# Fewer of the ten resident d_ff blocks for the early token chunks, weight conversion on another schedule, its clamp on VectorE

## The chip, the cores and the metric

One Trainium2 chip, one core. The metric is device time in microseconds of one execution. The time before is the median of three runs; the profile is of another single execution of the same program.

## The reference

Attention with a block-causal mask feeds a feed-forward layer with a rational activation. The weights `w_in` and `w_out` arrive as float64, everything else as float32.

```python
# q, k, v: 8 batches, 8 heads, 576 positions, 64 dims; blocks of 64 positions, block_i >= block_j
scores = (1 / sqrt(64)) * q @ k.T;  scores = where(mask, scores, -1e9)
attn = exp(scores - max);  attn = attn / (sum + 1e-9);  o = attn @ v
x = o.transpose(0, 2, 1, 3).reshape(4608, 512)          # tokens, d_model
h = x @ w_in                                            # d_ff = 2048
g = (a0 + a1*h + a2*h**2 + a3*h**3) / (1 + |b0|*|h| + |b1|*h**2 + 1e-6)
out = g @ w_out                                         # 4608 x 512 float32
```

## The kernel before

Every product is made with three matmuls of fp32r halves: each operand is split into a high part and a low part, and high x high, high x low and low x high are added up in PSUM.

**Attention** runs in 32 visits, one for each pair of heads of each batch, four visits to a batch. A visit has ten steps: five query tiles of growing key length (64 to 576 keys) for each of two heads. A step issues the score matmuls and the row maximum (`scores`); `expo` follows a step later, `transp` (division already done, transposes back into PSUM, split into halves) some ten steps later, and `pv` (the product with v) after the tiles 2 and 4. Its result is stored into a DRAM scratch `xscr`, from which the feed-forward part loads its tokens. Under a visit, `load` and `prep` fetch and transpose the next visit's q and k.

**Feed-forward** is cut into units. d_ff has 16 blocks of 128. In phase 0 a chunk has 256 tokens and a unit two blocks; in phase 1 a chunk has 512 tokens and a unit one block. Before, phase 0 takes blocks 0 to 9 for all 18 chunks (5 units each, 90 in all), phase 1 blocks 10 to 15 for all 9 chunks (6 units each, 54 in all). The weights of blocks 0 to 9 are resident in SBUF from the start on (`wpool`); those of 10 to 15 are converted into DRAM (`wscr`) and loaded when the attention's buffers are free. A unit passes `first` (24 or 12 matmuls into PSUM, and the first half of the polynomial), one unit later `recip`, then `split` (halves of g) and `second` (12 matmuls with N = 512). Phase 0 stores partial sums to `pscr`; phase 1 adds them and stores the output. The PSUM tile of `first` has one buffer in phase 0; the working tiles u, v, s have two.

**Weight conversion.** A step of `split_weights` loads 128 x 512 float64 values as pairs of 32-bit words and builds the high and the low half from their bits in `place`: an absolute value on ScalarE, a clamp on GpSimd (line 130), five bit operations on VectorE (132 to 139), a conversion of the low word on ScalarE (141), and two writes of the halves, on ScalarE and GpSimd for the resident blocks (144, 145), with DMAs for the others (147 to 149). There are 20 such steps for the resident blocks and 12 for the others. They use the working tiles u, v, s of the feed-forward part and its output staging tile `os`.

**Order.** The program interleaves by attention step. Conversions of the resident blocks stand at steps 9, 18, 27, 36 and then one at each step from 44 to 59; those of the others come at equal distances from step 80 to 230. Units begin at step 53, where the first batch's attention is complete, at a pace of a quarter of a half-unit per step for 40 steps, then evenly, so that 72 units are due at step 333. `ready` holds them behind the tokens that exist. The tile framework then orders each engine's queue by a timeline of its own, with what is ready earliest first, so an instruction can run ahead of its written place when its inputs and buffers allow it.

Lines that the prediction uses: 122 (fetch of weights), 130 to 149 (conversion), 207 (first product), 214 to 219, 224, 229 to 232 (activation), 239 and 240 (halves of g), 257 (second product), 432 to 437 (scores and maximum), 449 (exponential), 462 (division), 481 to 487 (transposes and their halves), 500 to 505 (product with v and its store).

Of the kernel before, what the change touches and what calls it, by code (L numbers as in the profile page):

```python
# [28 lines left out]
C0 = 0  # L29
# [6 lines left out]
W0 = 36  # L36
WA = 44
WD = 4
WB0 = 80
WBN = 150  # L40
UP = 25
UN = 40
# [7 lines left out]
NU = (NFA // NBU[0], NFB // NBU[1])  # L50
NCS = (NT // CTS[0], NT // CTS[1])
LP = 96
# [9 lines left out]
def attn_ffn_kernel(  # L62
# [52 lines left out]
    def split_weights(pool, f0, nf, dt):  # L115
        wih, wil, woh, wol = weight_tiles(pool, f0, nf, dt)

        def place(dhi, dlo, src, nm):

            nd, n = src.shape[1:]  # L120
            st = ffn.tile([128, 512, 2], I32, name=f"st{nm}", tag="os")
            nc.sync.dma_start(out=st.rearrange("p (d f) t -> p d (f t)", d=nd), in_=src.bitcast(I32))
            w0, w1 = st[:, :, 0], st[:, :, 1]
# [5 lines left out]
            nc.scalar.activation(out=at, in_=w1.bitcast(F32), func=AF.Abs)  # L129
            nc.gpsimd.tensor_scalar_max(at, at, WMIN)  # L130

# [6 lines left out]
            nc.vector.tensor_scalar(out=pi, in0=w0, scalar1=9, scalar2=None, op0=ALU.logical_shift_right)  # L138
# [12 lines left out]
        def steps():  # L151
            for f in range(0, nf, 2):
                cs = slice(f * 128, f * 128 + 256)
                for d in range(0, 4, 2):
                    src = w_in[d * 128:(d + 2) * 128, (f0 + f) * 128:(f0 + f + 2) * 128]
                    place(wih[:, d:d + 2, cs], wil[:, d:d + 2, cs],
                          src.rearrange("(d p) f -> p d f", p=128), f"i{f0}_{f}_{d}")
                    yield
                for d in range(f, f + 2):
                    place(woh[:, d:d + 1, :], wol[:, d:d + 1, :],  # L160
                          w_out[(f0 + d) * 128:(f0 + d + 1) * 128, :].rearrange("(d p) e -> p d e", p=128),
                          f"o{f0}_{d}")
                    yield

        return (wih, wil, woh, wol), steps()


    class Ffn:
# [26 lines left out]
        def first(self, ph, c, u):  # L195
            wih, wil, _, _ = self.w[ph]
# [5 lines left out]
            for j in range(NBU[ph]):  # L202
                f = NBU[ph] * u + j
                fs = slice(f * 128, (f + 1) * 128)
# [39 lines left out]
        def second(self, ph, c, u):  # L244
            _, _, woh, wol = self.w[ph]
            gh, gl = self.g.pop((ph, c, u))
            nu = NU[ph]
# [4 lines left out]
            for j in range(NBU[ph]):  # L252
                f = NBU[ph] * u + j
                for m in range(nm):
                    ms = slice(m * 128, (m + 1) * 128)
                    for i, (g, w) in enumerate(((gl, woh), (gh, woh), (gh, wol))):
                        nc.tensor.matmul(self.o[m], lhsT=g[:, j, ms], rhs=w[:, f, :],  # L257
                                         start=(u == 0 and j == 0 and i == 0),
                                         stop=(u == nu - 1 and j == NBU[ph] - 1 and i == 2))
            if u == nu - 1:  # L260
# [17 lines left out]
        def steps(self):  # L278
            units = [(ph, c, u) for ph in range(2) for c in range(NCS[ph]) for u in range(NU[ph])]
            l1, l2, l3 = LAG  # L280
            for i in range(len(units) + l3):
# [9 lines left out]
                if i < len(units):  # L291
                    ph, c, u = units[i]
                    self.first(ph, c, u)
                    if u == NU[ph] - 1:
# [14 lines left out]
    with ExitStack() as actx:  # L309
# [239 lines left out]
        for _ in range(C0):  # L549
            next(wsteps)  # L550
# [17 lines left out]
        NWA, NWB = 2 * NFA, 2 * NFB  # L568
        wdone = C0
        WSTEPS = [0] * C0 + [(W0 * (i + 1)) // 4 for i in range(4 - C0)] + [WA + WD * i // 4 for i in range(NWA - 4)]  # L570

        LAST = ALAG3 + 3
        there = [(6 * NPAIR + LAST, 1)] if G1 else []
        there += [((b + 1) * KB + LAST, ((b + 1) * S) // CT) for b in range(B)]
        E0, E1, U1 = there[0][0], there[-2][0], there[-2][1] * NU[0] * 2 - HOLD
        for step in attn_steps():

            wgoal = sum(step >= x for x in WSTEPS) + max(0, min(NWB, NWB * (step - WB0) // WBN))
            while wdone < wgoal:
                next(wsteps if wdone < NWA else wstepsB)  # L580
                wdone += 1
            while there and step >= there[0][0]:
                ff.ready = there.pop(0)[1]
            if step >= E0:
                goal = min(ff.ready * NU[0] * 2, (step - E0 + 1) * UP // 100 if step < E0 + UN else
                           (UN * UP // 100 + (U1 - UN * UP // 100) * (step - E0 - UN + 1) // (E1 + KB - E0 - UN)))
# [45 lines left out]
```

## Time and profile before

| | |
|---|---|
| median of three runs | 1383.16 us (1382.53 to 1386.95) |
| span of the profiled execution | 1379.1 us |
| mean granted TensorE clock | 0.974 |
| busy: TensorE matmul, weight load | 1278.1 us (93%), 1149.6 us (83%) |
| busy: VectorE, ScalarE, GpSimd | 1027.2 (74%), 909.4 (66%), 958.2 us (69%) |
| DMA | 200.84 MB, mean 146 GB/s |

The profiled execution has no run time of its own beside the span; the span runs from its first to its last instruction, and the runs' median is 4.1 us more. In the views PE is TensorE's matmul, PEld its weight load, DVE VectorE, ACT ScalarE, POOL GpSimd and SP SyncE; "L207" is line 207 of the kernel. A row of a group ends with: busy us, mean ns of one, idle time of the engine before them and what ended it. A matmul's shown duration contains its passage through the array, so neighbouring matmuls overlap; the distance of their starts is what one costs.

### The profile page before, as it was taken

The page shows a single profiled execution, that of the slowest core. Times are in us where ns is not written, and L with a number is a line of the kernel's source. Part 1 is how long each engine was busy: PE and PEld are TensorE (multiplying, and loading weights), DVE is VectorE, ACT ScalarE, POOL GpSimd, SP SyncE. Part 2 cuts the span into 40 slices and gives each one's busy share as a digit, 9 for nine tenths or more (in the row PEclk, how much of TensorE's full clock was granted, in tenths as well). Part 3 has the DMA queues.
Part 4 walks back from the last instruction along what each step waited for, and adds up shares of the span by engine and source line. Part 5 has one row for each costly group of instructions (what it writes and reads, how often), then busy time and mean ns, then how long its engine had stood idle before and what let it go on. Part 6 is the DMA issues. An engine that isn't in the chain of part 4 may idle for free.

```text
span 1379.1 us, 24416 instructions
## 1 busy us (share of the span) xinstructions
PE 1278.1 (93%) x8088; PEld 1149.6 (83%) x8088; DVE 1027.2 (74%) x2048; ACT 909.4 (66%) x2250; POOL 958.2 (69%) x1240
## 2 busy tenths in 40 slices
PE   4677899999899979999999999999989999999997
PEld 3667788999888879888998999998979888888885
DVE  5898877787778857887767777776676767676675
ACT  4766767777677756777767777776645655555553
POOL 4889987687678747777767676666556666666654
PEclk9788999999999999999999999999999999999999
DMA  9778556666556655665654555652632233333332
GB/s 216 198 196 238 146 150 166 168 166 181 148 145 150 164 151 132 165 166 153 157 140 123 154 134 122 160 127 65 213 141 77 77 123 123 122 123 123 122 113 86
DMA packets 216925, 200.84 MB, mean 146 GB/s; under 512 B 129504, under 2 KB 184800, under 8 KB 216800
## 3 DMA queue, kind: packets, MB, share of 16 engines
q1 hardware_dynamic: 216736, 199.28, 53.6%
q8 instruction: 65, 1.06, 0.3%
q14 instruction: 60, 0.49, 0.1%
q0 software_dynamic: 64, 0.00, 0.0%
HBM read 98.57 MB, written 44.04 MB: 103 GB/s over the span
## 4 chain that ended last, share of the span: by engine, by line
PE 69%; DVE 9%; POOL 9%; DMA 5%; ACT 3%; issue 3%; SPq 1%; POOLq 0%; DVEq 0%; ACTq 0%
PE h L207 25%; PE o L257 24%; PE o L500 8%; PE t L481 4%; PE s L432 3%; PE s L433 2%; PE tp L366 2%; POOL gl L240 1%; POOL p L462 1%; DMA x<-xscr 1%; POOL u L217 1%; DVE v L231 1%; DVE nm L437 1%; POOL v L216 1%; DMA xscr<-x 1%
## 5 line engine op out<-in xcount | busy, mean ns | idle before, releaser
L207 PE MATMUL h<-x,wih 128*128 128x256 f32 (+1 forms) x1872 | 415.7, 313 | 9.0 <-DMA x<-xscr 7.9
L207 PEld LDWEIGHTS h<-x,wih 128*128 128x128 f32 x1872 | 309.7, 191 | 29.1 <-issue 6.6
L207 PE MATMUL h<-x,wil 128*128 128x256 f32 (+1 forms) x936 | 290.7, 311 | 0.0
L240 POOL TENSOR_TENSOR gl<-s,gh 128x512 fp32r<-128x512 f32 x144 | 188.8, 1313 | 106.4 <-ACT gh L239 103.0
L257 PE MATMUL o<-woh,gl 128*128 128x512 f32 x576 | 232.2, 403 | 12.1 <-POOL gl L240 10.6
L257 PE MATMUL o<-wol,gh 128*128 128x512 f32 x576 | 227.7, 396 | 0.0
L257 PE MATMUL o<-woh,gh 128*128 128x512 f32 x576 | 227.7, 395 | 0.0
L437 DVE TENSOR_REDUCE nm<-s 128x1 f32<-128x288 f32 (+4 forms) x384 | 161.7, 427 | 78.4 <-PE s L436 45.2
L449 ACT ACTIVATE p<-s,nm 128x288 f32<-128x288 f32 (+4 forms) x384 | 184.9, 485 | 48.3 <-DVE nm L437 35.0
L217 POOL TENSOR_TENSOR u<-v,u 128x512 f32<-128x512 f32 x144 | 189.6, 1317 | 9.8
L216 POOL TENSOR_SCALAR v<-u,bab 128x512 f32<-128x512 f32 x144 | 118.9, 826 | 98.1 <-ACT u L214 94.6
L207 PEld LDWEIGHTS h<-x,wil 128*128 128x128 f32 x936 | 178.7, 191 | 8.7
L462 POOL TENSOR_SCALAR p<-p,rc 128x128 f32<-128x128 f32 (+3 forms) x256 | 164.8, 655 | 29.6 <-DVE rc L457 27.7
L218 DVE TENSOR_TENSOR s<-s,h 128x512 f32<-128x512 f32 x144 | 98.5, 684 | 100.1 <-ACT s L215 99.4
L432 PE MATMUL s<-kq 128*128 128x256 f32 (+3 forms) x384 | 137.3, 360 | 24.3 <-DMA kq<-hl 8.9
L224 ACT ACTIVATE v<-u,qcb 128x512 f32<-128x512 f32 x144 | 104.6, 726 | 69.6 <-POOL u L217 68.9
L214 ACT ACTIVATE u<-h 128x512 f32<-128x512 f32 x144 | 85.9, 596 | 94.2 <-PE h L207 90.1
L239 ACT CAST gh<-s 128x512 fp32r<-128x512 f32 x144 | 89.2, 623 | 82.1 <-DVE s L232 81.5
L257 PEld LDWEIGHTS o<-woh,gl 128*128 128x128 f32 x576 | 109.2, 190 | 35.5 <-POOL gl L240 14.3
L257 PEld LDWEIGHTS o<-wol,gh 128*128 128x128 f32 x576 | 109.1, 189 | 22.2
L257 PEld LDWEIGHTS o<-woh,gh 128*128 128x128 f32 x576 | 109.3, 190 | 18.9
L433 PE MATMUL s<-kq 128*128 128x256 f32 (+3 forms) x384 | 120.1, 315 | 0.0
(105 smaller groups left out, 3043.5 us busy)
## 6 DMA issues: line engine op xcount, KB each, us to landing
kq<-hl SPq DMA_DIRECT2D x64, 432.0 KB, 4.3
kq<-hl SPq DMA_DIRECT2D x64, 288.0 KB, 5.3
x<-xscr SPq DMA_DIRECT2D x56, 256.0 KB, 4.2
xscr<-x SPq DMA_DIRECT2D x32, 320.0 KB, 4.7
qr<-in_q_dram SPq DMA_DIRECT2D x64, 144.0 KB, 2.9
kr<-in_k_dram SPq DMA_DIRECT2D x64, 144.0 KB, 3.0
kq<-hl SPq DMA_DIRECT2D x64, 144.0 KB, 4.8
pscr<-os SPq DMA_DIRECT2D x18, 512.0 KB, 2.9
```

Of the source, the lines that this page charges most:

```text
L207: nc.tensor.matmul(h[:, j, :], lhsT=w[:, dc, fs], rhs=xs[dc][:, hl, :], start=(dc == 0 and i == 0), stop=(dc == 3 and i == 2))
L216: nc.gpsimd.tensor_scalar(out=vt, in0=ut, scalar1=b1, scalar2=b0, op0=ALU.mult, op1=ALU.add)
L217: nc.gpsimd.tensor_tensor(out=ut, in0=vt, in1=ut, op=ALU.mult)
L224: nc.scalar.activation(out=vt, in_=ut, func=AF.Ln, bias=qcb)
L240: nc.gpsimd.tensor_tensor(out=gl.rearrange("p j t -> p (j t)"), in0=st, in1=gh.rearrange("p j t -> p (j t)").bitcast(F32), op=ALU.subtract)
L257: nc.tensor.matmul(self.o[m], lhsT=g[:, j, ms], rhs=w[:, f, :], start=(u == 0 and j == 0 and i == 0), stop=(u == nu - 1 and j == NBU[ph] - ...
L432: nc.tensor.matmul(ps[:, :ww], lhsT=kq[:, 0, qs], rhs=kq[:, 1, c0:c0 + ww], start=True, stop=False)
L433: nc.tensor.matmul(ps[:, :ww], lhsT=kq[:, 0, qs], rhs=kq[:, 2, c0:c0 + ww], start=False, stop=not last)
L437: nc.vector.reduce_max(out=nm[:nq, j, i:i + 1], in_=ps[:nq, :w], axis=AX.X, negate=True)
L449: nc.scalar.activation(out=pt[:nq, j, c0:c0 + w], in_=banks[i][:nq, :w], func=AF.Exp, bias=nm[:nq, j, 0:1], scale=1.0, accum_out=sm[:nq, j ...
L462: nc.gpsimd.tensor_scalar(out=pt[:nq, jj, 64:n], in0=pt[:nq, jj, 64:n], scalar1=rc[:nq, jj:jj + 1], scalar2=1.0, op0=ALU.mult, op1=ALU.mult)
L500: nc.tensor.matmul(o[:, s0:w], lhsT=vblock(vv, x), rhs=pp, start=(x == 0 and i == 0), stop=(x == nb - 1 and i == 2))
```

## The change

Phase 0's units per chunk become a list: 2, 2, 3, 3, 4, 4 and then 5 for the other twelve chunks (4, 4, 6, 6, 8, 8 and then 10 blocks), 78 units in all. Phase 1 takes what is left of each pair of chunks: 12, 10 and 8 units for the first three, then 6 each, 66 in all; those of the first three chunks begin with resident blocks. Conversion steps are split into a fetch and a `place`, the fetch three attention steps ahead. Their places become a written list from step 4 to 164 for the resident blocks, and equal distances from step 176 to 312 for the others. Units are due by straight lines: 4 by step 93, 10 by step 133, 18 by step 173, 60 by step 333. The clamp moves to VectorE, and two instructions of `place`, the absolute value on ScalarE and the shift of the low word on VectorE, are pinned in the queue behind what the program has issued on their engine before them. The rest of the diff carries the unit count and the block numbers through `first`, `second` and `steps`.

```diff
@@ -26,20 +26,14 @@
 ALAG2 = 1
 LEND = 4
 RL = 3
-C0 = 0
 KQB = 3
 XB = 3
 HOLD = 6
 ALAG3 = 10
 OFFS = {5:(0,3,5)}
 G1 = 0
-W0 = 36
-WA = 44
-WD = 4
-WB0 = 80
-WBN = 150
-UP = 25
-UN = 40
+WB0 = 176
+WBN = 136
 LAG = (1, 2, 3)
 GBUFS = 2
 CBUFS = 2
@@ -47,8 +41,8 @@
 NFB = NF - NFA
 
 CTS, NBU = (CT, 512), (2, 1)
-NU = (NFA // NBU[0], NFB // NBU[1])
 NCS = (NT // CTS[0], NT // CTS[1])
+UA = (2, 2, 3, 3, 4, 4) + (5,) * 12
 LP = 96
 NL = S // LP
 QSCALE = 0.125
@@ -115,27 +109,29 @@
     def split_weights(pool, f0, nf, dt):
         wih, wil, woh, wol = weight_tiles(pool, f0, nf, dt)
 
-        def place(dhi, dlo, src, nm):
-
-            nd, n = src.shape[1:]
+        def fetch(src, nm):
+            nd = src.shape[1]
             st = ffn.tile([128, 512, 2], I32, name=f"st{nm}", tag="os")
             nc.sync.dma_start(out=st.rearrange("p (d f) t -> p d (f t)", d=nd), in_=src.bitcast(I32))
+            return st
+
+        def place(dhi, dlo, st, nd, nm):
             w0, w1 = st[:, :, 0], st[:, :, 1]
             at = ffn.tile([128, 512], F32, name=f"wa{nm}", tag="u")
             bt = ffn.tile([128, 512], F32, name=f"wb{nm}", tag="v")
             pt = ffn.tile([128, 512], F32, name=f"wp{nm}", tag="s")
             ai, bi, pi = at.bitcast(I32), bt.bitcast(I32), pt.bitcast(I32)
 
-            nc.scalar.activation(out=at, in_=w1.bitcast(F32), func=AF.Abs)
-            nc.gpsimd.tensor_scalar_max(at, at, WMIN)
-
+            tc.keep_in_program_order(nc.scalar.activation(out=at, in_=w1.bitcast(F32), func=AF.Abs))
+            nc.vector.tensor_scalar_max(at, at, WMIN)
             nc.vector.tensor_scalar(out=ai, in0=ai, scalar1=3, scalar2=0x3FFFF000,
                                     op0=ALU.logical_shift_left, op1=ALU.bitwise_and)
             nc.vector.scalar_tensor_tensor(out=bi, in0=w1, scalar=-0x40000000, in1=ai,
                                            op0=ALU.bitwise_and, op1=ALU.bitwise_or)
 
             nc.vector.tensor_scalar(out=ai, in0=bi, scalar1=-0x800000, scalar2=None, op0=ALU.bitwise_and)
-            nc.vector.tensor_scalar(out=pi, in0=w0, scalar1=9, scalar2=None, op0=ALU.logical_shift_right)
+            tc.keep_in_program_order(nc.vector.tensor_scalar(out=pi, in0=w0, scalar1=9, scalar2=None,
+                                                             op0=ALU.logical_shift_right))
             nc.vector.scalar_tensor_tensor(out=pi, in0=w1, scalar=23, in1=pi,
                                            op0=ALU.logical_shift_left, op1=ALU.bitwise_or)
             nc.scalar.activation(out=pt, in_=pt.bitcast(U32), func=AF.Copy, scale=2.0 ** -43)
@@ -153,17 +149,25 @@
                 cs = slice(f * 128, f * 128 + 256)
                 for d in range(0, 4, 2):
                     src = w_in[d * 128:(d + 2) * 128, (f0 + f) * 128:(f0 + f + 2) * 128]
-                    place(wih[:, d:d + 2, cs], wil[:, d:d + 2, cs],
-                          src.rearrange("(d p) f -> p d f", p=128), f"i{f0}_{f}_{d}")
+                    st = fetch(src.rearrange("(d p) f -> p d f", p=128), f"i{f0}_{f}_{d}")
+                    yield
+                    place(wih[:, d:d + 2, cs], wil[:, d:d + 2, cs], st, 2, f"i{f0}_{f}_{d}")
                     yield
                 for d in range(f, f + 2):
-                    place(woh[:, d:d + 1, :], wol[:, d:d + 1, :],
-                          w_out[(f0 + d) * 128:(f0 + d + 1) * 128, :].rearrange("(d p) e -> p d e", p=128),
-                          f"o{f0}_{d}")
+                    st = fetch(w_out[(f0 + d) * 128:(f0 + d + 1) * 128, :].rearrange("(d p) e -> p d e", p=128),
+                               f"o{f0}_{d}")
                     yield
+                    place(woh[:, d:d + 1, :], wol[:, d:d + 1, :], st, 1, f"o{f0}_{d}")
+                    yield
 
         return (wih, wil, woh, wol), steps()
 
+
+    def nu(ph, c):
+        return NF - 2 * UA[2 * c] if ph else UA[c]
+
+    def blocks(ph, c, u):
+        return [2 * UA[2 * c] + u] if ph else [2 * u, 2 * u + 1]
 
     class Ffn:
         def __init__(self):
@@ -193,15 +197,14 @@
                 self.x[ph, c] += [x[:, d] for d in range(nd)]
 
         def first(self, ph, c, u):
-            wih, wil, _, _ = self.w[ph]
             xs = self.x[ph, c]
             tag = f"{ph}_{c}_{u}"
             pool = self.pools[self.n % len(self.pools)]
             hp = self.hpools[self.n % len(self.hpools)]
             h = hp.tile([128, NBU[ph], CTS[ph]], F32, name=f"h{tag}", tag="a", bufs=1 if hp is ps_h else 3)
-            for j in range(NBU[ph]):
-                f = NBU[ph] * u + j
-                fs = slice(f * 128, (f + 1) * 128)
+            for j, f in enumerate(blocks(ph, c, u)):
+                wih, wil, _, _ = self.w[f // NFA]
+                fs = slice(f % NFA * 128, (f % NFA + 1) * 128)
                 for dc in range(4):
                     for i, (w, hl) in enumerate(((wih, 1), (wih, 0), (wil, 0))):
                         nc.tensor.matmul(h[:, j, :], lhsT=w[:, dc, fs], rhs=xs[dc][:, hl, :],
@@ second, steps
...
-            for j in range(NBU[ph]):
-                f = NBU[ph] * u + j
+            for j, f in enumerate(blocks(ph, c, u)):
+                _, _, woh, wol = self.w[f // NFA]
...
-            units = [(ph, c, u) for ph in range(2) for c in range(NCS[ph]) for u in range(NU[ph])]
+            units = [(ph, c, u) for ph in range(2) for c in range(NCS[ph]) for u in range(nu(ph, c))]
...
@@ -546,8 +548,6 @@
 
         wts, wsteps = split_weights(wpool, 0, NFA, F32R)
         load(0)
-        for _ in range(C0):
-            next(wsteps)
         prep(0, 0)
         prep(0, 1)
         vprep(0)
@@ -565,26 +565,27 @@
 
         KB = NPAIR * 10
         wscr, wstepsB = split_weights(dpool, NFA, NFB, F32)
-        NWA, NWB = 2 * NFA, 2 * NFB
-        wdone = C0
-        WSTEPS = [0] * C0 + [(W0 * (i + 1)) // 4 for i in range(4 - C0)] + [WA + WD * i // 4 for i in range(NWA - 4)]
+        at_ = [4, 12, 20, 28, 42, 46, 50, 54, 64, 72, 80, 88, 100, 109, 118, 127, 140, 148, 156, 164]
+        at_ += [WB0 + WBN * i // (2 * NFB) for i in range(2 * NFB)]
+        WSTEPS = sorted([(k, 1) for k in at_] + [(max(0, k - 3), 0) for k in at_])
+        wall = (x for g in (wsteps, wstepsB) for x in g)
 
         LAST = ALAG3 + 3
-        there = [(6 * NPAIR + LAST, 1)] if G1 else []
-        there += [((b + 1) * KB + LAST, ((b + 1) * S) // CT) for b in range(B)]
-        E0, E1, U1 = there[0][0], there[-2][0], there[-2][1] * NU[0] * 2 - HOLD
+        there = [((b + 1) * KB + LAST, ((b + 1) * S) // CT) for b in range(B)]
+        E0, E1 = there[0][0], there[-2][0]
+        UC = lambda n: 2 * sum(UA[:n])
+        PACE = [(E0, 0), (E0 + KB, UC(2)), (E0 + 2 * KB, UC(4)), (E0 + 3 * KB, UC(6)),
+                (E1 + KB, UC(there[-2][1]) - HOLD)]
         for step in attn_steps():
 
-            wgoal = sum(step >= x for x in WSTEPS) + max(0, min(NWB, NWB * (step - WB0) // WBN))
-            while wdone < wgoal:
-                next(wsteps if wdone < NWA else wstepsB)
-                wdone += 1
+            while WSTEPS and step >= WSTEPS[0][0]:
+                WSTEPS.pop(0)
+                next(wall)
             while there and step >= there[0][0]:
                 ff.ready = there.pop(0)[1]
             if step >= E0:
-                goal = min(ff.ready * NU[0] * 2, (step - E0 + 1) * UP // 100 if step < E0 + UN else
-                           (UN * UP // 100 + (U1 - UN * UP // 100) * (step - E0 - UN + 1) // (E1 + KB - E0 - UN)))
-                emit(max(0, goal - done))
+                (s0, u0), (s1, u1) = next(((x, y) for x, y in zip(PACE, PACE[1:]) if step < y[0]), PACE[-2:])
+                emit(max(0, min(UC(ff.ready), u0 + (u1 - u0) * (step - s0 + 1) // (s1 - s0)) - done))
 
     wB = ctx.enter_context(tc.tile_pool(name="wB", bufs=1))
     ffb = ctx.enter_context(tc.tile_pool(name="ffb", bufs=2))
```

More of the change, by code (lines that the diff above doesn't have):

```diff
@@ L244, in second @@
         def second(self, ph, c, u):
-            _, _, woh, wol = self.w[ph]
             gh, gl = self.g.pop((ph, c, u))
-            nu = NU[ph]
+            last = u == nu(ph, c) - 1
             nm = CTS[ph] // 128
@@ L256, in second @@
                     for i, (g, w) in enumerate(((gl, woh), (gh, woh), (gh, wol))):
-                        nc.tensor.matmul(self.o[m], lhsT=g[:, j, ms], rhs=w[:, f, :],
+                        nc.tensor.matmul(self.o[m], lhsT=g[:, j, ms], rhs=w[:, f % NFA, :],
                                          start=(u == 0 and j == 0 and i == 0),
-                                         stop=(u == nu - 1 and j == NBU[ph] - 1 and i == 2))
-            if u == nu - 1:
+                                         stop=(last and j == NBU[ph] - 1 and i == 2))
+            if last:
                 for k in range(nm // 2):
@@ L293, in steps @@
                     self.first(ph, c, u)
-                    if u == NU[ph] - 1:
+                    if u == nu(ph, c) - 1:
                         self.x.pop((ph, c))
```

## The prediction

> **What bounds the kernel now.** I read the busy shares first, then the busy times of six stretches with the granted clock, then the groups of instructions inside the stretches, then single visits, then single instructions. A step is the score matmul of one head of one query tile, ten steps make a visit (one pair of heads) and 320 the attention. The cuts come from the score matmuls' start times: step 0 starts at 17.5 us, step 53 at 145.9, step 173 at 515.9, and the attention's last matmuls end near 968 to 980.
>
> ```profile
> PE 1278.1 (93%) x8088; PEld 1149.6 (83%) x8088; DVE 1027.2 (74%) x2048; ACT 909.4 (66%) x2250; POOL 958.2 (69%) x1240
> ```
>
> TensorE looks like the bound everywhere. The stretches say otherwise:
>
> ```profile
> core 0: us, PE busy (x) PEld busy (x) DVE busy (x) ACT busy (x) POOL busy (x), PEclk, DMA share, GB/s
> 17.50:145.90 128.40, 92.84 (x539) 82.98 (x540) 109.53 (x260) 88.60 (x269) 109.55 (x146) 0.81 0.81 211
> 145.90:515.90 370.00, 341.70 (x2419) 315.91 (x2417) 288.82 (x624) 259.70 (x715) 276.32 (x389) 0.99 0.62 158
> 515.90:700.00 184.10, 178.44 (x1281) 165.45 (x1280) 146.95 (x318) 134.72 (x366) 141.06 (x200) 1.00 0.60 150
> 700.00:968.00 268.00, 265.57 (x1912) 247.98 (x1912) 194.73 (x435) 195.53 (x525) 182.89 (x284) 1.00 0.52 129
> 968.00:1065.00 97.00, 91.08 (x586) 82.78 (x585) 65.20 (x82) 52.96 (x88) 56.52 (x45) 0.96 0.40 143
> 1065.00:1379.10 314.10, 304.17 (x1341) 251.21 (x1339) 214.81 (x314) 172.27 (x279) 186.05 (x167) 0.99 0.34 114
> ```
>
> Take length minus busy time times clock as what TensorE loses: 53.2 us in the first row, 31.7 in the second, then 5.7, 2.4, 9.6 and 13.0. TensorE's work is nearly the same in both kernels, so the change can only win or lose in these losses. The first row holds the largest. There TensorE is not the bound: VectorE and GpSimd are both busy 85% of the time (109.5 of 128.4), and weight conversions fill them:
>
> ```profile
> L130 POOL TENSOR_SCALAR wai<-wai 128x512 f32<-128x512 f32 x9 | 15.4, 1710 | 1.5 <-ACT wai L129 1.1
> L130 POOL TENSOR_SCALAR wao<-wao 128x512 f32<-128x512 f32 x8 | 13.1, 1641 | 0.6 <-ACT wao L129 0.3
> L145 POOL TENSOR_TENSOR wil<-wpi,wai 128x512 fp32r<-128x512 f32 x9 | 11.6, 1295 | 4.4 <-ACT p L449 4.3
> L145 POOL TENSOR_TENSOR wol<-wpo,wao 128x512 fp32r<-128x512 f32 x8 | 10.2, 1270 | 0.7 <-DVE wao L137 0.5
> L134 DVE SCALAR_TENSOR_TENSOR wbi<-sti,wai 128x512 int32<-128x512 int32 x10 | 8.3, 833 | 0.0
> L132 DVE TENSOR_SCALAR wao<-wao 128x512 int32<-128x512 int32 x8 | 3.7, 468 | 1.1 <-POOL wao L130 1.1
> ```
>
> These are the first stretch's groups: 17 conversions. On VectorE there are ten such groups (the first and the last are shown) with 59.4 us, 3.5 us a conversion; on GpSimd 50.3 us, of which the clamp (L130) is 28.5, 1.68 us each. By the written schedule only 4 conversions belong before step 44; the trace shows that the planner had pulled them some 25 steps forward.
>
> **The change, part by part.** The plan after has conversions at steps 4, 12, 20, 28, 42, 46 and 50 in the first stretch (7 for 17), 13 from step 54 to 164 in the second (10 ran there before), and 12 from step 176 to 300 in the rest (4 before; one before 17.5 us). The pin holds a conversion's first instruction behind what ScalarE has already been given, so it cannot run ahead. Early chunks have 2, 2, 3, 3, 4, 4 units, so 18 units are due by step 173.
>
> ```profile
> L207 PE MATMUL h<-x,wih 128*128 128x256 f32 x29 | 6.3, 315 | 0.1
> ...
> L207 PE MATMUL h<-x,wih 128*128 128x256 f32 x484 | 96.3, 292 | 7.9 <-DMA x<-xscr 7.9
> ...
> L207 PE MATMUL h<-x,wih 128*128 128x256 f32 x685 | 135.8, 290 | 0.1
> ```
>
> With 16 of these to a unit, the first stretch has under 2 units, the second 30, the rest of the attention 43. After: 0, 18, some 44. The planner drew units about 5 ahead of their pace; after it can hardly do so before step 163, since the chunks' tokens are not there.
>
> *First stretch.* VectorE: 109.5 - 59.4 + 7 x 4.1 = 78.8 us. The 4.1 is 3.5 plus the clamp's new place, priced at 0.6 from the mean of the other one-input VectorE instructions (0.47 to 0.88 in this stretch). GpSimd: 109.6 - 50.3 + 7 x 1.28 = 68. At the same 85% VectorE needs 92 us. A visit's chain also has a length of its own:
>
> ```profile
> 17.50:34.70 17.20, 10.08 (x51) 8.18 (x52) 12.77 (x36) 11.60 (x38) 10.13 (x17) 0.92 1.00 232
> 87.50:108.70 21.20, 17.10 (x102) 15.77 (x103) 19.88 (x48) 17.10 (x54) 19.88 (x28) 0.76 0.82 210
> 108.70:136.30 27.60, 21.69 (x137) 19.88 (x135) 24.13 (x53) 18.52 (x54) 24.65 (x32) 0.81 0.86 235
> ```
>
> Visit 0, which has nobody's transposes before it, took 17.2 us; visit 3, with some three conversions, 21.2; visit 4, with more, 27.6. With 1.3 conversions a visit I take 20 us: 17.2 + 4.3 x 20 = 103, so 25 us shorter. About 5 us of unit work (43 first matmuls at 0.12) go to later: -20. Ends: 92 us (-31) and 24 a visit (-2). I take the value nearest to visit 3.
>
> *Second stretch.* Twelve units leave. A unit costs TensorE 24 x 0.120 + 12 x 0.227 = 5.6 us:
>
> ```profile
> 944.92 0.40 PE L207 MATMUL h<-x,wih 128*128 128x256 f32 x2
> 945.16 0.28 PE L207 MATMUL h<-x,wil 128*128 128x256 f32 x1
> ...
> 1109.63 0.39 PE L257 MATMUL o<-woh,gl 128*128 128x512 f32 x1
> 1109.86 0.39 PE L257 MATMUL o<-woh,gh 128*128 128x512 f32 x1
> ```
>
> and VectorE five instructions, 3.9 us:
>
> ```profile
> L218 DVE TENSOR_TENSOR s<-s,h 128x512 f32<-128x512 f32 x144 | 98.5, 684 | 100.1 <-ACT s L215 99.4
> L219 DVE SCALAR_TENSOR_TENSOR s<-s,coef,h 128x512 f32<-128x512 f32 x144 | 107.0, 743 | 2.4
> L230 DVE SCALAR_TENSOR_TENSOR u<-u,v 128x512 f32<-128x512 f32 x90 | 72.1, 802 | 27.3 <-ACT v L229 25.9 <-POOL vpl L394 0.8
> L231 DVE SCALAR_TENSOR_TENSOR v<-u,v 128x512 f32<-128x512 f32 x90 | 74.2, 824 | 1.1
> L232 DVE SCALAR_TENSOR_TENSOR s<-s,coef,v 128x512 f32<-128x512 f32 x90 | 78.1, 868 | 1.2
> ```
>
> VectorE after: 288.8 - 12 x 3.9 - 10 x 3.5 + 13 x 4.1 = 260 us; TensorE's work 338.3 - 67 = 271. VectorE is then nearly level with TensorE, and at the first stretch's 85% it sets 305 us. That is 65 shorter for 67 us of work moved to later: +2. Ends: at 90% VectorE and 94% TensorE 289 (-14), at 80% 325 (+22). So taking units away here buys almost nothing by itself: the stretch only changes its bound.
>
> *From step 173 to the attention's end.* TensorE is the bound and eight conversions are added. Between 515.9 and 700 us four conversions stand beside 5.7 us lost, between 700 and 968 none beside 2.4, so one costs (5.7 - 2.4 x 184/268) / 4 = 1.0 us. Single visits give more:
>
> ```profile
> 628.30:660.70 32.40, 29.43 (x208) 27.11 (x208) 26.64 (x57) 22.98 (x63) 25.03 (x35) 1.00 0.50 125
> 660.70:689.60 28.90, 28.90 (x223) 27.58 (x222) 22.79 (x50) 22.31 (x60) 22.07 (x33) 1.00 0.67 162
> ```
>
> The first of these, with one conversion, loses 3.0, the second, without, nothing. I take the mean over the long stretch: 8 x 1.0 = +8; ends 0 and +24.
>
> *The units that change phase.* Twelve units of 5.6 us become twelve of 24 x 0.227 = 5.45: -2. The twelve join the last phase, where VectorE (215 of 314 us) and GpSimd (186) have room. The loads ahead of use cost nothing as long as a staging buffer is free: 512 KB each, as before, under the attention's matmuls; if both are taken by a chunk's output, the fetch stands at the head of SyncE's queue and the next visit's q and k loads behind it. The end of the last phase and the join at 1024 us keep their loss.
>
> Sum: -20 + 2 + 8 - 2 = -12 us on a span of 1379.1, 1367. The runs' median, 1383.2, is 4.1 over the span of the profiled execution; so 1371.
>
> **The rivals.** *The clamp on VectorE collides with GpSimd (slower).* A one-input VectorE instruction that meets a GpSimd one takes far longer:
>
> ```profile
> 558.96 1.29 POOL L240 TENSOR_TENSOR gl<-s,gh 128x512 fp32r<-128x512 f32 x1
> 559.02 1.52 DVE L132 TENSOR_SCALAR wai<-wai 128x512 int32<-128x512 int32 x1 [0.20 <-POOL wai L130]
> 562.67 0.40 DVE L137 TENSOR_SCALAR wai<-wbi 128x512 int32<-128x512 int32 x1
> ```
>
> 1.52 us beside L240, 0.40 alone. If the clamp and the mask behind it both meet one each time, a conversion takes 2.2 us more of VectorE; in the second stretch, where VectorE is level with the bound, that is 13 x 2.2 / 0.85 = +34: span 1401, time 1405. It decides from about 0.8 us a conversion on. Against it: the mean of such instructions is 0.47 to 0.88. The Trainium skill states the same cause: its GPSIMD Engine Reference, Key points, says that GpSimd shares its SBUF interfaces with VectorE and contends with VectorE instructions in a 2-port mode or with two SBUF inputs. The trace agrees in the 1.52 against 0.40; by the rule taken strictly, with GpSimd busy 75% of the second stretch, the clamp would be dear there, and this rival would hold.
>
> *The early visits have a length of their own.* If a visit takes 24 us even with one conversion (visit 4 took 27.6 with both engines near 90%), the first term is -2: 1385 span, 1389.
>
> *VectorE and GpSimd really were all that held the early part.* Then the ends hold, -31, -14 and 0, with -2: span 1332, time 1336. For it: both engines are equally full in the first row, and the clamp's 28.5 us leave the fuller chain.
>
> *The clock.* The first row has 0.81. Fewer units could spread that into the second stretch: 271 us of work at 0.9 would need 301, just below VectorE's 305. So this adds nothing until the clock falls below 0.89. By the Trainium skill (TensorE: Matmul & The Clock Gate, What's actually happening) the clock halves after an idle window of about 3.4 us; no wait of that length is expected with TensorE busy 88%, and the second row's 0.99 at 92% agrees.
>
> **How the numbers follow.** Forecast 0.55; clamp 0.15; long visits 0.17; full gain 0.13. A change of under 0.3% (4 us) is about what a measurement of this kernel cannot tell from none. The forecast's own spread puts 0.51 of its 0.55 faster, 0.03 level and 0.01 slower; the long visits are level with 0.08 and slower with 0.09. Faster 0.64, same 0.11, slower 0.25. The range reaches to 1345, most of the way to the full gain, and to 1396, beyond the long visits and short of the full clamp rival. The likeliest case alone holds 1360 to 1382.
>
> **What would show it.** First stretch: step 53 near 120 us, with about 7 conversions, GpSimd busy under 70%. Second: step 173 near 425 us with some 18 units done and VectorE busy about 85%, TensorE near 88%. Then visits near 31 to 33 us with a conversion in most. The clamp's group on VectorE near 0.6 us. Wrong would be: step 53 not before 138 us, or the clamp and L132's successor over 1 us in the mean, or visits over 34 us after step 173.

## The result and the profile after

The changed kernel takes 1438.85 us (median of four runs, 1435.25 to 1441.69) against 1385.06 us for the kernel before: 1.039 times the time, interval 1.0361 to 1.0419. The forecast of 1371 us, its range and its sign were wrong. The profiled execution's span is 1433.5 us against 1379.1, so 54.4 us have to be found.

The busy shares of the page after:

```profile
PE 1305.9 (91%) x7944; PEld 1167.0 (81%) x7944; DVE 1038.8 (72%) x2080; ACT 912.6 (64%) x2250; POOL 897.7 (63%) x1208
```

GpSimd got 60 us of work less and VectorE 12 us more, as the diff says. Both have a smaller share than before, and still the run is longer. The same six stretches, cut at step 0, step 53, step 173, a round time, the end of the attention and the join, show where (columns as in the table before):

```profile
core 0: us, PE busy (x) PEld busy (x) DVE busy (x) ACT busy (x) POOL busy (x), PEclk, DMA share, GB/s
19.20:129.00 109.80, 83.02 (x521) 76.35 (x521) 71.50 (x205) 70.02 (x231) 55.78 (x115) 0.86 0.78 189
129.00:482.60 353.60, 302.13 (x1987) 277.81 (x1986) 266.22 (x598) 237.33 (x676) 218.42 (x347) 0.88 0.63 157
482.60:700.00 217.40, 210.70 (x1490) 195.00 (x1488) 177.46 (x392) 158.80 (x435) 152.85 (x232) 0.98 0.64 165
700.00:947.00 247.00, 234.02 (x1656) 216.57 (x1656) 186.90 (x409) 174.00 (x465) 174.27 (x248) 0.99 0.56 144
947.00:1065.00 118.00, 113.42 (x701) 102.14 (x700) 81.52 (x98) 62.91 (x105) 73.26 (x59) 0.99 0.35 123
1065.00:1433.50 368.50, 358.31 (x1579) 295.84 (x1577) 250.08 (x366) 205.18 (x331) 219.02 (x197) 0.99 0.29 95
```

The prediction's measure, length minus TensorE's busy time times its clock, gives the loss of each. It is good to some 4 us in the longest rows, since the clock has two places and is a mean over the stretch, not over TensorE's busy time.

| stretch | loss before | loss after | difference | predicted |
|---|---|---|---|---|
| steps 0 to 53 | 53.2 | 38.4 | -14.8 | -20 |
| steps 53 to 173 | 31.7 | 87.7 | +56.0 | +2 |
| step 173 to the attention's end | 8.1 | 26.2 | +18.1 | +8 |
| to the join | 9.6 | 5.7 | -3.9 | 0 |
| last phase | 13.0 | 13.8 | +0.8 | 0 |

Together +56.2. Step 0 begins 1.7 us later, and the twelve units that change phase save 12 x (24 x 0.120 - 12 x 0.227) = 1.9 us of matmuls by the prediction's distances. That makes 56.0 for the 54.4, which is within the error. So the question is the second row. Its +56.0 has two parts: TensorE's idle time grew by 23.2 us (51.5 for 28.3), and the lower clock costs 36.3 us of its busy time for 3.4, which is 32.8 more.

In that stretch VectorE is busy 266.2 of 353.6 us, 75%, and TensorE 85% at a clock of 0.88. No engine is full. The longest waits of TensorE there, after and then before (total, times, longest):

```profile
PE s L434 <- DMA kq<-hl: 11.8, 5, 4.6
PE o L502 <- DVE pt0l L489: 8.7, 5, 2.6
PE tp L368 <- DMA kr<-in_k_dram: 4.7, 4, 2.7
```

```profile
PE h L207 <- DMA x<-xscr: 7.9, 3, 3.0
PE o L500 <- DVE pt0l L487: 4.9, 4, 2.1
PE tp L366 <- ACT p L449: 3.7, 3, 1.6
```

They now belong to the steps of a visit: the copy of q and k, the transposed probabilities, the load of k. None is large by itself.

### The profile page after: what moved, and what is told of

Read it like the earlier page. It is cut to its first block, busy times and chain, and to the rows that moved or that the text cites. A ratio compares the mean times of both kernels' runs of the same rounds, so it can differ in the third digit from the quotient of the medians.

```text
span 1433.5 us, 24128 instructions
## 1 busy us (share of the span) xinstructions
PE 1305.9 (91%) x7944; PEld 1167.0 (81%) x7944; DVE 1038.8 (72%) x2080; ACT 912.6 (64%) x2250; POOL 897.7 (63%) x1208
## 4 chain that ended last, share of the span: by engine, by line
PE 68%; DVE 11%; DMA 8%; ACT 4%; POOL 3%; issue 3%; SPq 2%; POOLq 0%; DVEq 0%; ACTq 0%
PE h L210 25%; PE o L259 23%; PE o L502 8%; DMA kq<-hl 5%; PE t L483 4%; PE s L434 3%; PE s L435 3%; PE tp L368 2%; DVE nm L439 1%; DMA kr<-in_k_dram 1%; DVE pt2l L489 1%; POOL gl L243 1%; ACT p L451 1%; DVE s L221 1%; DVE u L233 1%
## 5 line engine op out<-in xcount | busy, mean ns | idle before, releaser
L210 PEld LDWEIGHTS h<-x,wih 128*128 128x128 f32 x1776 | 302.7, 194 | 34.5 <-DMA x<-xscr 3.4
L210 PE MATMUL h<-x,wil 128*128 128x256 f32 (+1 forms) x888 | 284.3, 320 | 0.0
L259 PE MATMUL o<-woh,gl 128*128 128x512 f32 x576 | 229.3, 398 | 6.1 <-POOL gl L243 5.2
L220 POOL TENSOR_TENSOR u<-v,u 128x512 f32<-128x512 f32 x144 | 192.9, 1339 | 9.7
L434 PE MATMUL s<-kq 128*128 128x256 f32 (+3 forms) x384 | 145.0, 379 | 51.6 <-DMA kq<-hl 38.5
L464 POOL TENSOR_SCALAR p<-p,rc 128x128 f32<-128x128 f32 (+3 forms) x256 | 161.7, 644 | 39.9 <-DVE rc L459 37.5
L210 PEld LDWEIGHTS h<-x,wil 128*128 128x128 f32 x888 | 172.5, 194 | 10.7
L434 PEld LDWEIGHTS s<-kq 128*128 128x128 f32 x384 | 79.0, 206 | 64.4 <-issue 42.0
L483 PE MATMUL t<-ident,p 128*128 128x128 f32 (+1 forms) x672 | 116.0, 286 | 14.7 <-ACT p L451 5.9
```

The costliest lines, as they stand in the source:

```text
L210: nc.tensor.matmul(h[:, j, :], lhsT=w[:, dc, fs], rhs=xs[dc][:, hl, :], start=(dc == 0 and i == 0), stop=(dc == 3 and i == 2))
L220: nc.gpsimd.tensor_tensor(out=ut, in0=vt, in1=ut, op=ALU.mult)
L259: nc.tensor.matmul(self.o[m], lhsT=g[:, j, ms], rhs=w[:, f % NFA, :], start=(u == 0 and j == 0 and i == 0), stop=(last and j == NBU[ph] - ...
L434: nc.tensor.matmul(ps[:, :ww], lhsT=kq[:, 0, qs], rhs=kq[:, 1, c0:c0 + ww], start=True, stop=False)
L464: nc.gpsimd.tensor_scalar(out=pt[:nq, jj, 64:n], in0=pt[:nq, jj, 64:n], scalar1=rc[:nq, jj:jj + 1], scalar2=1.0, op0=ALU.mult, op1=ALU.mult)
L483: nc.tensor.transpose(ps[:, i, :nq], src, ident[:nq, :nq])
```

## The experiments

Theories, numbered as the expectations name them: 1, the copy of q and k to its three buffers has become the bound; 2, the pins hold up queues; 3, the clamp (3a in the later runs), and 3b the conversions as a whole, lengthen VectorE's chain; 4, any edit gives a new order of instructions, and that alone costs 10 to 30 us; 5, conversions and units collide in shared tiles; 6, an early visit has a length of its own, and the units taken away had only filled it; 7, the late conversions are dear; 8, a load three steps ahead holds a staging tile too long. Each ratio is to the kernel before on the same chip at the same time and carries a 95% interval.

### One part of the change at a time

`units_only`: the kernel before with the changed units and their pace.

```
+UA = (2, 2, 3, 3, 4, 4) + (5,) * 12      # and PACE as in the change
 places: 9, 18, 27, 36, 44, 45, ... 59, then from 80 on, as before; load at the place; clamp on GpSimd; no pins
```

> The kernel before with the new unit list and pace alone (2, 2, 3, 3, 4, 4 and then 5 units); conversions at their old steps, unpinned, clamp on GpSimd. Theory 1, copy loop: the second copy of a visit's q and k halves can only be issued when the third kq buffer comes free near the end of the visit before, takes 6 to 8 us and is used at once, so a visit does not get below 26 to 29 us when units are taken away from it: 1430 to 1455 us, steps 53 to 173 take over 340 us with about 17 units. Theory 2, pinned conversions in every visit hold the queues: 1375 to 1392 us. Theory 3, clamp on VectorE: 1375 to 1392 us.

Measured 1398.1 against 1383.6, 1.0105 (1.0088 to 1.0122).

`style_only`: the changed kernel with the units, their pace and the places of the conversions as before; what is left of the change are the pins, the load three steps ahead and the clamp on VectorE.

```
-UA = (2, 2, 3, 3, 4, 4) + (5,) * 12
+UA = (5,) * 18
 places: 9, 18, 27, 36, 44, 45, ... 59, then from 80 on
+PACE = [(E0, 0), (E0 + 40, 10), (E1 + KB, UC(there[-2][1]) - HOLD)]
```

> The new way of converting (fetch ahead, two pins, clamp on VectorE) at the old steps and with the old units (5 a chunk). Theory 1: 1372 to 1398 us, since no unit is taken from a visit. Theory 2: 1410 us or more, the pins hold ScalarE and VectorE at places where 16 conversions follow each other. Theory 3: 1395 to 1415 us.

Measured 1402.4, 1.0131 (1.0114 to 1.0148).

`clamp_only`: the kernel before, one line changed.

```
-            nc.gpsimd.tensor_scalar_max(at, at, WMIN)
+            nc.vector.tensor_scalar_max(at, at, WMIN)
```

> The kernel before with the clamp on VectorE and nothing else. Theories 1 and 2: 1370 to 1387 us; 28 us of GpSimd leave the first stretch, where it is busy 85%, and VectorE gets some 10. Theory 3: 1395 us or more, the clamp's mean on VectorE near 1.2 us.

Measured 1413.6, 1.0215 (1.0199 to 1.0230).

`units_only` costs 14.5 us, `style_only` 18.8, the whole change 53.8: some 20 us are in neither alone. They belong to the new places of the conversions or to the parts meeting. The second stretch of `units_only` has the changed kernel's units and 31 us less length; below it that of `style_only`, which has 27 units and 19 conversions, since its pins hold back nine that the kernel before ran in the first stretch:

```profile
143.80:466.50 322.70, 286.69 (x1982) 258.40 (x1981) 234.53 (x560) 224.63 (x654) 225.59 (x353) 0.97 0.70 180
129.00:511.70 382.70, 345.18 (x2305) 315.55 (x2305) 312.33 (x679) 268.51 (x728) 270.45 (x380) 0.93 0.63 161
```

Their losses are 44.6 and 61.7 us for 31.7 before. So in this stretch the units alone cost 12.9 us and the new way of converting alone 30.0; the other 13 of the 56.0 come only with the whole change. Compare steps 93 to 173, `style_only` and then the changed kernel:

```profile
259.80:511.60 251.80, 239.40 (x1683) 221.79 (x1681) 199.65 (x430) 179.36 (x486) 179.35 (x257) 0.98 0.63 160
```

```profile
244.80:482.60 237.80, 204.61 (x1375) 188.45 (x1374) 176.67 (x394) 159.84 (x453) 145.22 (x231) 0.91 0.62 155
```

`style_only` does 308 matmuls more over the same 80 steps, 8.6 units or 48 us of work by the prediction's 5.6 us a unit, in only 14.0 us more (with 6 conversions for 8). Those units fill time that the changed kernel leaves idle.

### Undoing one part of the changed kernel

`after_no_pins` takes both pins away:

```
-            tc.keep_in_program_order(nc.scalar.activation(...)); tc.keep_in_program_order(nc.vector.tensor_scalar(...))
+            nc.scalar.activation(...); nc.vector.tensor_scalar(...)
```

> The changed kernel without its two pins; the planner may draw conversions forward again. Theory 1: 1425 to 1450 us, the units are missing in steps 53 to 173 as before. Theory 2: under 1415 us.

`after_clamp_pool` puts the clamp back:

```
-            nc.vector.tensor_scalar_max(at, at, WMIN)
+            nc.gpsimd.tensor_scalar_max(at, at, WMIN)
```

> The changed kernel with the clamp back on GpSimd. Theory 1 (starved visits wait for the copy into the third kq buffer): 1425 to 1445 us, the starved stretch keeps its loss. Theory 3a (the clamp on VectorE lengthens each conversion's run of VectorE instructions, between which the scores' maxima have to wait; it cost 30 us alone): 1405 to 1420 us. Theory 4 (each new order that the planner finds lies 10 to 30 us above the order of the kernel before, whatever is changed): 1415 to 1450 us with no tie to the clamp.

`fetch_at_place` loads at the conversion's own step:

```
-        WSTEPS = sorted([(k, 1) for k in at_] + [(max(0, k - 3), 0) for k in at_])
+        WSTEPS = sorted([(k, 1) for k in at_] + [(k, 0) for k in at_])
```

> The changed kernel with each fetch at its conversion's step and not three steps ahead. Theory 8 (the fetched words hold one of the two staging tiles that the chunks' outputs need): steps 173 to the attention's end lose 10 to 20 us less, 1415 to 1428 us. Otherwise 1430 to 1450 us.

Measured 1433.0 (1.0356, 1.0332 to 1.0380), 1427.7 (1.0334, 1.0307 to 1.0361) and 1428.9 (1.0322, 1.0279 to 1.0365). Each gives back 6 to 11 us of 54. None is the cause of the whole; theories 2 and 8 fall as main causes of the total. Their second stretches, in the same order, say more than the totals:

```profile
138.70:474.50 335.80, 294.01 (x1982) 265.86 (x1981) 255.82 (x580) 229.20 (x663) 209.23 (x340) 0.94 0.64 161
126.30:465.70 339.40, 291.80 (x1953) 265.02 (x1952) 253.95 (x580) 232.28 (x669) 236.66 (x359) 0.93 0.65 161
128.40:472.20 343.80, 298.47 (x1997) 273.54 (x1997) 265.33 (x602) 239.06 (x678) 219.85 (x349) 0.91 0.64 160
```

The loss there is 59.4, 68.0 and 72.2 us for 87.7, so each part of the new way of converting has a share in it, the pins the largest (28 us). The shares add up to more than the 56.0, so they overlap. Other stretches take part of it back: without pins the first stretch is 10 us longer (119.9), with the clamp on GpSimd the third (474.5 for 464.4).

### The copy of q and k (theory 1)

A fourth buffer needs space. `alias` makes it by keeping no low half of the resident output weights (its products read the high half in its place) and is the control; `alias_kqb4` and `alias_kqb4_hl2` add buffers.

```
 alias:            wol = [128, 1, DM] scratch; in second: wol = woh for f < NFA
 alias_kqb4:       -KQB = 3   +KQB = 4
 alias_kqb4_hl2:   and two buffers for hl, the copy's source
```

> The changed kernel, with the low half of w_out left out for the resident blocks (the high half is used in its place, so the output lacks that term; the same instructions run). It is the control for the next two and frees 18 KB a partition. All theories: within 12 us of the changed kernel, 1427 to 1450 us.

> As the control (low half of w_out left out for the resident blocks), with four kq buffers for three. Theory 1: the second copy of the next visit goes out before the current visit's last scores; the TensorE loss in steps 53 to 173 falls from about 105 us to under 75, and the time to 1385 to 1412 us. Theories 3a and 4: no tie to the buffer, 1425 to 1450 us.

> As the one with four kq buffers, and two buffers for the halves of q and k from which the copies are made. Theory 1, if the next link of the same chain is the halves' buffer: another 5 to 20 us less than with four kq buffers alone; if not, within 8 us of it. Theories 3a and 4: 1425 to 1450 us.

Measured 1434.7 (1.0385, 1.0353 to 1.0417), 1443.0 (1.0445, 1.0398 to 1.0492) and 1438.4 (1.0411, 1.0386 to 1.0437). The wait that theory 1 blames went down from 10.6 to 2.3 us. Waits of TensorE in the second stretch, `alias` and then `alias_kqb4`:

```profile
PE s L439 <- DMA kq<-hl: 10.6, 5, 4.0
PE o L507 <- DVE pt0l L494: 8.7, 5, 2.6
```

```profile
PE o L507 <- DVE pt0l L494: 13.2, 7, 3.2
PE h L214 <- DMA x<-xscr: 5.7, 2, 4.9
...
PE s L439 <- DMA kq<-hl: 2.3, 1, 2.3
```

The probabilities took its place, and the stretch hardly moved, 352.6 to 348.7 us:

```profile
127.20:475.90 348.70, 297.24 (x1969) 271.84 (x1969) 260.98 (x596) 234.68 (x671) 218.22 (x347) 0.90 0.62 159
```

Theory 1 falls: the wait was where the idle time showed, not why it was there.

### The conversions' chain (theories 3 and 5)

`no_dve_conv` and `before_no_dve` take every VectorE instruction out of the conversions, in both kernels. ScalarE keeps two of its three passes and GpSimd its product; in the kernel before GpSimd's clamp goes too.

```
-            the Abs on ScalarE, the clamp, the five VectorE instructions, the scaling on ScalarE
+            nc.scalar.copy(out=bt, in_=w1.bitcast(F32))
-            nc.gpsimd.tensor_tensor(..., in0=v3(pt), in1=v3(at), op=ALU.mult)
+            nc.gpsimd.tensor_tensor(..., in0=v3(bt), in1=v3(bt), op=ALU.mult)
```

> The changed kernel with each conversion cut to a copy on ScalarE and one product on GpSimd, so that VectorE has none of its seven instructions (the weights are not the reference's). Theory 3a: at 14 conversions and some 5 us each in steps 53 to 173, that stretch falls from 354 to about 285 to 305 us and the time to 1350 to 1385 us. Theory 1 and the plain length of a visit: steps 53 to 173 keep over 325 us, since a visit's own chain sets it, and the time stays over 1400 us.

> The kernel before with each conversion cut to a copy on ScalarE and one product on GpSimd (the weights are not the reference's): what all conversions cost in the old arrangement; in the new one the same cut gave 28 us. Theory 6: steps 0 to 53 fall from 128 to about 110 us, as in the changed kernel, and the rest little: 1350 to 1368 us. Theory 3b: under 1345 us.

Measured 1410.0 (1.0190, 1.0161 to 1.0219) and 1356.8 (0.9820, 0.9771 to 0.9869). Steps 0 to 53, 53 to 173 and on to the attention's end, `no_dve_conv` and then `before_no_dve`:

```profile
18.70:129.10 110.40, 81.58 (x519) 74.88 (x520) 57.17 (x171) 67.33 (x228) 52.06 (x119) 0.83 0.78 193
129.10:463.30 334.20, 293.93 (x1999) 269.40 (x1998) 214.32 (x515) 229.44 (x659) 201.48 (x346) 0.93 0.66 165
463.30:924.90 461.60, 441.88 (x3136) 411.15 (x3135) 323.86 (x724) 324.51 (x886) 308.21 (x476) 0.99 0.60 154
```

```profile
17.20:132.20 115.00, 84.03 (x521) 75.55 (x521) 57.78 (x170) 79.17 (x250) 60.97 (x127) 0.83 0.90 233
132.20:491.50 359.30, 343.09 (x2437) 319.17 (x2437) 253.10 (x576) 256.86 (x707) 246.63 (x380) 0.98 0.64 163
491.50:955.90 464.40, 457.48 (x3287) 426.32 (x3284) 337.30 (x746) 332.48 (x900) 320.29 (x483) 1.00 0.56 138
```

The part left out costs 28.9 us in the new arrangement (1438.9 - 1410.0) and 25.3 in the old (1382.1 - 1356.8): spreading the conversions out hid none of it. And without it the two kernels still stand 53 us apart, so VectorE's conversions do not explain the total, and theory 3 falls as the main cause. By stretches they do count: without them the kernels' losses in the second stretch differ by 37.8 us (60.9 and 23.1) and not 56.0, and the first stretch gains 2.6 (42.7 and 45.3) and not 14.8. The first row also says that 110 us is what the first five visits take with no conversion on VectorE at all.

`alias_own` gives the conversions tiles of their own in place of those that the units use:

```
-  tag="u", tag="v", tag="s"
+  tag="cu", tag="cv", tag="cs"            # in alias
```

> As the control without the low half of w_out for the resident blocks, with working tiles of their own for the conversions (two each of 2 KB), which before share u, v and s with the units. Theory 5 (a conversion among units is dear because it holds one of the two u, v, s buffers, so the units wait for each other): the loss in steps 53 to 173 falls by 20 us or more and the time to 1390 to 1418 us. Theory 3a (VectorE's in-order run of seven instructions is what delays the scores' maxima): within 10 us of the control, 1425 to 1445 us. Theory 4: 1420 to 1450 us, not tied to it.

Measured 1449.6, 1.0490 (1.0468 to 1.0511), 15 us above `alias`: theory 5 falls.

### The length of a visit (theory 6)

`no_units_early`: the changed kernel with no unit due in the early chunks.

```
-        PACE = [(E0, 0), (E0 + KB, UC(2)), (E0 + 2 * KB, UC(4)), (E0 + 3 * KB, UC(6)), ...]
+        PACE = [(E0, 0), (E0 + 3 * KB, 0), ...]
```

> The changed kernel with no unit due before step 173 (the rest of the pace unchanged). Theory 6 (a visit has a length of its own of some 21 us, 8 more than its TensorE work, and a unit put into it adds only 4 to 5 us of its 5.6): steps 53 to 173 take 255 to 285 us with under 4 units, and the time is 1440 to 1470 us, since 18 more units stand where no visit's idle time can hold them. Theory 3b (conversions set the length of these visits): over 300 us for steps 53 to 173.

Measured 1444.2 against 1382.1, 1.0445 (1.0388 to 1.0503). Its second stretch has one unit, 13 conversions and the same twelve visits:

```profile
130.80:388.80 258.00, 212.15 (x1371) 188.95 (x1369) 187.81 (x510) 179.82 (x575) 149.78 (x295) 0.88 0.74 184
```

Twelve visits with one unit take 258.0 us, 21.5 each, with no engine near full: this is theory 6's length of a visit. Followed back from its last instruction, the stretch's chain lies for a third in the attention's matmuls, for 17% in two transfers (the copy of q and k 11.4%, the load of k 5.6%), and for 18% on VectorE, with 5% on ScalarE.

What a unit adds to this is 36 matmuls and 5.6 us of TensorE's work. The changed kernel has 616 matmuls more, 17 units, and takes 353.6: 95.6 us, 5.6 each. Its early units hide nothing, not even the 0.6 to 1.6 us of each that theory 6 expected, and so it costs the whole run only a half per cent to have none of them. The kernel before has 29 units more than this row and takes 370.0 us, with ten conversions: 112 us, 3.8 each. Few units do not explain this by themselves, for `units_only` has 17 more and takes 322.7 us with its nine conversions: 64.7 us, again 3.8 each. What differs is how and where the conversions stand around the units. So theory 6 holds for the length of a visit, but not for the missing units as the whole cause. What the visits would take with the old conversions and no units was not measured, so 3.8 is a comparison and not the price of a unit.

### Later conversions, and edits that should do nothing (theories 7 and 4)

`late_b`: the kernel before with the twelve late conversions where the change puts them. `neutral_w0` and `neutral_hold`: the kernel before with one number moved.

```
 late_b:        -WB0 = 80    +WB0 = 176      -WBN = 150   +WBN = 136
 neutral_w0:    -W0 = 36     +W0 = 40
 neutral_hold:  -HOLD = 6    +HOLD = 5
```

> The kernel before with only the conversions of the blocks 10 to 15 moved, to steps 176 to 312. Theory 7 (these conversions cost TensorE 2 us each where it is the bound, whatever the rest): steps 173 to the attention's end lose 12 to 22 us more, steps 53 to 173 lose 5 to 15 less, and the time is 1380 to 1400 us. If they are free anywhere: within 15 us either way with no such exchange in the stretches.

> The kernel before with its first four conversions written at steps 10, 20, 30 and 40 for 9, 18, 27 and 36, and nothing else: same instructions, same buffers, another order from the planner in early visits. Theory 4 (any new order lies 10 to 30 us above this one, since this one was picked among many): 1393 to 1415 us. Theories 1, 3a and 5 (below): within 7 us of before, 1376 to 1390 us.

> The kernel before with one half-unit more due before the attention's end (HOLD 5 for 6), which shifts the pace from step 93 on by less than one half-unit. Theory 4: 1390 to 1415 us. Theories 1, 3a and 5: 1376 to 1390 us.

Measured 1398.6 (1.0118, 1.0086 to 1.0151), 1388.3 (1.0048, 1.0032 to 1.0063) and 1397.8 (1.0114, 1.0091 to 1.0137). The two stretches from step 53 on in `late_b`, and the second of them in the kernel before:

```profile
148.30:510.90 362.60, 342.40 (x2418) 319.19 (x2417) 255.01 (x582) 254.92 (x698) 240.59 (x373) 0.97 0.56 139
510.90:977.20 466.30, 450.16 (x3212) 416.78 (x3211) 373.64 (x797) 336.50 (x911) 360.61 (x498) 1.00 0.59 151
```

```profile
515.90:979.50 463.60, 455.50 (x3275) 424.22 (x3274) 350.13 (x765) 336.22 (x902) 329.04 (x487) 1.00 0.55 137
```

From step 173 on the loss is 16.1 for 8.1 us: eight conversions more, 1 us each, which is what the prediction took for them. The total rose by twice that, 16.5 us, as its last phase is longer (419.5 us from the attention's end for 399.6).

The edits that move one number cost 5.7 and 15.2 us, so theory 4 holds in part. An effect of up to some 15 us in the total is not told from a new order of the instructions here; the 54 us are. In the second stretch smaller effects can be told. In `neutral_w0` and `neutral_hold` it is

```profile
143.30:522.00 378.70, 350.30 (x2436) 322.57 (x2435) 290.61 (x632) 264.95 (x723) 275.68 (x396) 0.97 0.63 158
146.10:515.20 369.10, 345.01 (x2414) 319.79 (x2413) 286.54 (x623) 259.55 (x714) 275.40 (x390) 0.97 0.62 159
```

with losses of 38.9 and 34.4 us for 31.7, up to 7 us more. Each row is of one execution. The 12.9 of `units_only` is not far above this; the 30.0 of `style_only` and the 28 of the pins are.

## Why the prediction was wrong

**The first stretch: right, its size a third too large** (-20 for -14.8 of loss). Step 53 came at 129.0 us, against 145.9 before and a forecast near 120, with GpSimd busy 51%. The length fell by 18.6 to 109.8 where 103 was forecast. By the prediction's own sum (17.2 + 4.3 visits) that is 21.5 us a visit in place of 20, the same 21.5 that a visit without units has in the second stretch. Fewer conversions did shorten it, down to what `no_dve_conv` takes too (110.4).

**The second stretch: the step that failed.** "VectorE is then nearly level with TensorE, and at the first stretch's 85% it sets 305 us." The busy times in that sentence were good: 266 us for VectorE (260 forecast), 266 of TensorE's work (271). The step from busy time to length was not: 353.6 us, with VectorE at 75%. I took an engine's highest share elsewhere for a bound of the stretch, as if the work could always be packed that tightly. An early visit is a chain through TensorE, VectorE, ScalarE and two transfers, 21.5 us long with a conversion or so in it; the prediction had found this for the first stretch ("a visit's chain also has a length of its own") and dropped it for the second.

The term of +2 measured +56.0, 23.2 of it idle time and 32.8 the clock. The prediction's reason for it, twelve units leaving, cost 12.9 alone where it said "almost nothing". The rest is a cost that it put at nothing: it counted the conversions' busy time, gave the pins no price and called the load ahead free while a staging buffer is. The new way of converting cost 30.0 alone, with nine more conversions in the stretch, and taking the pins out of the changed kernel gave back 28. Why the conversions cost so much more this way, and why 13 us come only with both, stays open; the part that `no_dve_conv` leaves out makes some 18 of the 56.

**After step 173: sized too low,** +18.1 for +8. `late_b` bears out the 8. The other 10 are no smaller in `no_dve_conv` (24.1 us of loss in its last row), so they are not VectorE's; their cause stays open.

**The clamp rival: its mechanism fell.** The clamp's two groups on VectorE in the changed kernel (count, busy, mean ns):

```profile
L126 DVE TENSOR_SCALAR wao<-wao 128x512 f32<-128x512 f32 x16 | 8.5, 534 | 2.2 <-ACT wao L125 1.9
L126 DVE TENSOR_SCALAR wai<-wai 128x512 f32<-128x512 f32 x16 | 7.9, 496 | 3.8 <-ACT wai L125 3.6
```

0.52 us in the mean, not the 0.8 from which it decides, and the price of 0.6 was fair. In the second stretch none of the 13 clamps took over 0.43 us. The Trainium skill (GPSIMD Engine Reference, Key points) has VectorE contend with GpSimd in a 2-port mode or with two SBUF inputs; the 0.52 us, with GpSimd busy 62% of the stretch, bears it out for single meetings at most. Yet the clamp's move does cost: 19.7 us of the second stretch's loss go when it is undone, and `clamp_only` costs 30 us in the old arrangement. The second stretch of `clamp_only` is 14 us longer than before, with VectorE no fuller than 75%:

```profile
150.30:534.20 383.90, 348.43 (x2417) 321.01 (x2414) 286.53 (x637) 260.81 (x714) 257.22 (x381) 0.96 0.61 153
```

30 us is twice what the dearer of the two neutral edits cost, and it is not explained.

**The long visits: right mechanism, wrong place.** That rival priced it in the first stretch alone, at +18 on the forecast.

**The full gain: fell.** The first stretch gave 14.8 of the 31 us, with both engines far from full (VectorE 65%, GpSimd 51%).

**The clock: wrong.** "So this adds nothing until the clock falls below 0.89": it fell to 0.88, and 12% of 302 us of busy time is 36 us, the larger part of the second stretch's loss beyond the 31.7 before. It does not follow the number of units: `no_units_early` has 0.88 too, but `units_only` 0.97 with as many units as the changed kernel, and `style_only` 0.93 with more. Whether the lower clock lengthens the visits or only fills their waits was not separated.

**What was right besides:** the last phase's loss (+0.8 for 0), 17 units finished and three more begun by step 173 for 18, and visits of 32 us afterwards for 31 to 33.

## What to carry to other kernels

An engine's busy share is not the capacity of a stretch: before work is moved out of one, ask what the rest takes by itself, dependencies and all. A run with the filler removed answers this in one row, and the length per added unit says whether a filler still hides (3.8 of 5.6 us among the old conversions here, 5.6 of 5.6 among the new). Read undoing runs by stretch: three that give back 6 to 11 us of the total give back 15 to 28 us of the stretch in question. Where the order of instructions comes from a planner, time an edit that should do nothing first. Its cost, here 6 to 15 us of the total and up to 7 us of the stretch, is the resolution of every other comparison.

## What was not expected of the hardware

TensorE's clock fell to half with no single long wait. In the second stretch of `no_units_early` the longest single wait is 2.5 us:

```profile
PE s L434 <- DMA kq<-hl: 14.3, 8, 2.5
PE s L434 <- ACT p L451: 4.5, 8, 1.4
```

and the clock is 0.88. Two of its drops, each with the 3.4 us before it:

```profile
170.50:173.90 3.40, 0.47 (x2) 0.30 (x2) 0.74 (x4) 0.84 (x4) 0.63 (x1) 1.00 0.61 142
173.90:187.60 13.70, 11.91 (x55) 11.34 (x56) 8.08 (x24) 7.62 (x26) 5.29 (x14) 0.50 0.49 120
235.30:238.70 3.40, 1.63 (x15) 1.40 (x14) 1.33 (x7) 2.80 (x12) 1.40 (x5) 1.00 0.54 147
238.70:248.90 10.20, 9.57 (x44) 8.96 (x44) 7.72 (x23) 6.01 (x19) 7.39 (x13) 0.50 0.62 127
```

Fifteen matmuls and 1.63 us of work in such a window did not keep the clock up; the next 10.2 us ran at half. The Trainium skill (TensorE: Matmul & The Clock Gate, What's actually happening) speaks of an idle window of about 3.4 us. The two drops here last 13.7 and 10.2 us, about four and three times that; but neither window was wholly idle, and the waits in it were short ones. How much work in a window would keep the clock up is not shown.
